# A gated linear attention with a feed-forward layer: the order of its pieces written anew, the state added by VectorE, the first logarithms split by ScalarE

## The chip, the cores and the metric

One core of one Trainium2 chip. The metric is the device time of one execution in microseconds (us), the median of the runs. Engines: TensorE (PE in the rows; PEld is its weight load), VectorE (DVE), ScalarE (ACT), GpSimd (POOL) and SyncE (SP), which issues most DMAs.

## The reference

```python
f = 1.0 / (1.0 + np.exp(-f_logit))            # B, H, S, D = 4, 8, 768, 48
for t in range(S):
    state = f[:, :, t, :, None] * state + einsum('bhd,bhe->bhde', k[:, :, t], v[:, :, t])
    y[:, :, t] = einsum('bhd,bhde->bhe', q[:, :, t], state)
x = y.transpose(0, 2, 1, 3).reshape(B * S, H * D)        # 3072 x 384
h = x @ w_in                                             # 384 -> 2048
out = (0.5 * (h + np.sqrt(h * h + 4.0))) @ w_out         # 2048 -> 384
```

## The kernel before, in words

The 3072 tokens are cut into 12 pairs of blocks, 256 tokens each, three pairs to a batch; a pair has two blocks of 128 tokens (cc = 0, 1), each on 64 partitions, two neighbouring tokens to a partition (i = 0, 1). All work is described as named pieces, `describe` makes them, and a table of words, ORDER, sets the order: the program emits the pieces in the order of the table. A word is the piece, the pair, a colon and the engine (A ScalarE, D VectorE, P GpSimd, S SyncE, T TensorE), for TensorE also the PSUM banks. So each engine takes its pieces in the table's order, and a piece that waits holds all that stands behind it on its engine.

The pieces of a pair p, with their lines in the kernel before:

- `lf`, `lq`, `lk`, `lv` (L171): loads of f, q, k, v, 384 KB each, issued by SyncE; `wi`, `wo` (L144, L149): the weights, issued by GpSimd.
- `ex` (L178): exp(-f). `ut` (L185): adds 1, into two of the three parts of the tile UT. `tt` (L138): their product. `ln` (L198, L202): its logarithm s. L138 is the helper of all multiplications, L133 and L135 of all copies.
- `hi`, `lo` (L208, L214): s as a fp16 high half and the remainder, in the tile hl. Pair 0 has none of both: it is in the list DIRECT, and its prefix sums run on the fp32 s32.
- `cu` (L234, L239): prefix sums of the logarithms by matmuls with a triangle, and sums of blocks. `c1` (L252, pairs 3 to 11): VectorE adds s for the second sum. `ep`, `ea`, `ge` (L262, L302): exponentials of the sums. `gs`, `gb` (L138): small factors of the state.
- `qu`, `ku`, `qm`, `km` (L138): q and k times factors. `vc`: v to fp16.
- `tp`, `te` or, for pairs 4 to 11, `tx` (L323): q and k transposed, on TensorE or by a DMA.
- `sc` (L364), `pm` (L371): scores and their mask. `kv` (L383): the pair's contribution to the state, in PSUM. `ia` (L394): a matmul of the old state sn with the identity, which adds it to `kv`'s result in PSUM. `sa`, `sb` (L401, L408): VectorE multiplies that sum with gs or gb, from PSUM, which gives the state for the next block.
- `yt` (L421), `yn` (L430): the output from within the block and from the state. `yc`: to fp16. `xp`, `xe` or, for pairs 4 to 11, `xx` (L445): y transposed.
- `m1` (L470), eight to a pair: h = y w_in, six matmuls each. `sq` (L479), `rt` (L485): square and square root on ScalarE. `gt` (L495): 0.5 h plus the root on VectorE. `m2` (L507), eight to a pair: four matmuls each of the output. `ev`, `st` (L527): copy and store.

Pair 0 is loaded and prepared in two halves of the heads (x = 0, 1: `ex0.0`, `ex0.1`). ScalarE switches between two tables of functions (the words TABLE:e and TABLE:s). The buffers of each tile rotate with the depths in DEPTH.

Of the kernel before, what the change touches and what calls it, by code (L numbers as in the profile page):

```python
# [31 lines left out]
ln2.0:A vc0.1:A lq2.0:S hi2.0:P pm0.00:D ep1.0:A gs0:P lo2.0:P ge1:A pm0.10:D vc0.0:A pm0.01:D ea1.0:A kv0:T@32 km1.0:P
ex3.0:A cu2.0:T@41 pm0.11:D lk2.0:S sa0:D yt0:T@60 ge2:A gs1:D yn0.1:T yc0.0:A qu1.0:D gb2:P lv1.0:S ep2.0:A qm1.0:D wi1:P
yc0.1:A ea2.0:A xp0.1:T@5 wi2:P xp0.0:T@7 ut3.0:D tp1.0:T@36 ex4.0:A lf5.0:S xe0.0:D tt3.0:P xe0.1:D te1.0.0:A te1.1.0:D
m1.0.0:T@4 wo3:P ln3.0:A ut4.0:D m1.0.1:T@0 wi3:P sq0.0:A qu2.0:D sc1.1:T@17 sq0.1:A hi3.0:P pm1.11:D TABLE:s rt0.0:A lo3.0:P
m1.0.2:T@5 pm1.10:D ia0.1:T lv2.0:S gb1:D cu3.0:T@3 tt4.0:D ku2.0:P sc1.0:T@67 sb0:D m1.0.3:T@1 pm1.00:D sq0.2:A pm1.01:D
# [5 lines left out]
pm2.01:D m1.1.5:T@0 hi4.0:P sq1.1:A lv3.0:S gt0.7:D lo4.0:P yt2:T@47 rt1.0:A gt0.6:D yn2.1:T m1.1.2:T@2 hi5.0:P sq1.3:A
gt1.1:D wo5:P m2.0.00:T@5 lf6.0:S sq1.2:A yc2.1:D m2.0.10:T@1 ku5.0:P rt1.1:A gt1.0:D m1.1.7:T@7 sq1.5:A gt1.3:D m1.1.6:T@3
sq1.7:A lo5.0:P yn2.0:T gt1.2:D lq4.0:S m2.0.11:T sq1.6:A km3.0:D m1.1.4:T@6 wo7:P rt1.3:A xp2.1:T@2 lf7.0:S m2.0.12:T wo6:P
qu3.0:D sq1.4:A m2.0.01:T xe2.1:D qm3.0:P yc2.0:A gt1.7:D cu4.0:T@2 rt1.2:A gt1.6:D xp2.0:T@4 m2.0.02:T TABLE:e ge4:A xe2.0:D
cu5.0:T@7 ku4.0:P gt1.4:D tp3.0:T@34 lq5.0:S c14.0:D m1.2.2:T@6 ex6.0:A te3.0.0:D m2.0.13:T vc3.0:P ep5.0:A gt1.5:D lf8.0:S
# [9 lines left out]
ev2.0:A ut9.0:D kv4:T@15 gb7:P st1.01.0:S sq3.0:A ia4.0:T tt8.0:D m2.2.12:T gs5:P ep7.0:A pm4.10:D m2.2.13:T ln8.0:A tt9.0:P
lq8.0:S sq3.1:A sa4:D yt4:T@32 gb5:P ln9.0:A ev2.1:D yn4.0:T vc5.0:P yn4.1:T lf11.0:S TABLE:s rt3.0:A m1.3.3:T@6 yc4.0:D
qu7.0:P yc4.1:D ia4.1:T sc5.0:T@17 sb4:D xx4:S kv5:T@32 qm6.0:P pm5.01:D ia5.0:T m1.3.2:T@5 sq3.3:A sa5:D m1.3.5:T@7 sq3.2:A
gt3.0:D km6.0:P m1.3.6:T@3 rt3.1:A gt3.1:D ia5.1:T m1.3.7:T@4 pm5.00:D sq3.5:A m1.3.4:T@2 gt3.2:D sq3.7:A ku7.0:P lk9.0:S
sc5.1:T@01 gt3.3:D sq3.4:A m2.3.10:T@5 st2.01.1:S rt3.2:A pm5.10:D lv7.0:S m1.4.2:T@6 pm5.11:D st1.01.1:S hi9.0:P m2.3.11:T  # L60
# [586 lines left out]
```

## Time and profile before

| | |
|---|---|
| median of 3 runs | 206.72 us (206.17 to 207.64) |
| the profiled execution | 205.34 us |
| its span, first to last instruction | 203.6 us |
| TensorE, VectorE, ScalarE, GpSimd busy | 177.7, 147.3, 154.9, 108.6 us |
| mean granted TensorE clock | 0.954 |
| moved by DMA | 32.87 MB, mean 161 GB/s |

Busy time is the time in which an engine has work, not work at its best: a busy share over the whole span is a mean over stages. Waits are what an engine stood idle for and what ended it. The chain is followed back from the last instruction, at each step to what released it. The clock row is in tenths of 2.4 GHz, 40 slices of 5.09 us.

### The profile page before, as it was taken

The page shows a single profiled execution, that of the slowest core. Times are in us where ns is not written, and L with a number is a line of the kernel's source. Part 1 is how long each engine was busy: PE and PEld are TensorE (multiplying, and loading weights), DVE is VectorE, ACT ScalarE, POOL GpSimd, SP SyncE. Part 2 cuts the span into 40 slices and gives each one's busy share as a digit, 9 for nine tenths or more (in the row PEclk, how much of TensorE's full clock was granted, in tenths as well). Part 3 has the DMA queues.
Part 4 walks back from the last instruction along what each step waited for, and adds up shares of the span by engine and source line. Part 5 has one row for each costly group of instructions (what it writes and reads, how often), then busy time and mean ns, then how long its engine had stood idle before and what let it go on. Part 6 is the DMA issues. An engine that isn't in the chain of part 4 may idle for free.

```text
span 203.6 us, 5630 instructions
## 1 busy us (share of the span) xinstructions
PE 177.7 (87%) x2302; PEld 129.1 (63%) x2302; DVE 147.3 (72%) x285; ACT 154.9 (76%) x248; POOL 108.6 (53%) x135
## 2 busy tenths in 40 slices
PE   0556898799899999979999979789998999999990
PEld 0544575587657766757667857467775778677660
DVE  7649579999688997957978958818984778434650
ACT  4266679999958999769988987758886698968700
POOL 4226789899969979929679738695000000000001
PEclk9995579999999999999999999969999999999998
DMA  6999999999959799994899999932894100505305
GB/s 158 269 262 244 275 198 217 234 256 273 183 156 234 108 254 203 222 278 99 129 214 207 249 129 240 195 51 36 149 140 119 39 5 0 42 0 155 77 22 136
DMA packets 80537, 32.87 MB, mean 161 GB/s; under 512 B 73888, under 2 KB 80496, under 8 KB 80512
## 3 DMA queue, kind: packets, MB, share of 16 engines
q1 hardware_dynamic: 76688, 29.27, 69.1%
q0 software_dynamic: 3824, 3.24, 9.9%
q8 instruction: 18, 0.29, 0.6%
q14 instruction: 7, 0.06, 0.1%
HBM read 25.17 MB, written 4.72 MB: 147 GB/s over the span
## 4 chain that ended last, share of the span: by engine, by line
issue 32%; PE 26%; POOL 18%; DMA 15%; ACT 3%; DVE 2%; SPq 2%; POOLq 0%
PE ps L507 10%; POOL qk L138 6%; PE ps L470 6%; DMA q<-in_q_dram 4%; PE ps L234 4%; POOL k L138 4%; DMA xT<-y 3%; DMA wout<-in_moe_w_out_dram 3%; DMA v<-in_v_dram 2%; POOL wout L149 2%; DMA f<-in_f_logit_dram 2%; POOL v L135 2%; POOL hl L214 2%; PE ps L364 1%; PE ps L383 1%
## 5 line engine op out<-in xcount | busy, mean ns | idle before, releaser
L470 PE MATMUL ps<-xT,win 128*128 128x256 f16 x576 | 74.0, 277 | 5.1 <-DMA xT<-y 3.5
L495 DVE SCALAR_TENSOR_TENSOR g<-ps,r 128x512 f16<-128x512 f32 x96 | 62.2, 682 | 17.5 <-ACT r L485 17.3
L507 PE MATMUL ps<-wout,g 128*128 128x384 f16 x384 | 71.6, 326 | 2.4 <-DMA wout<-in_moe_w_out_dram 1.3
L479 ACT ACTIVATE hsq<-ps 128x512 f16<-128x512 f32 x96 | 54.7, 593 | 18.0 <-PE ps L470 17.3
L470 PEld LDWEIGHTS <-win 128*128 128x128 f16 x576 | 55.5, 99 | 17.2 <-DMA xT<-y 4.2
L485 ACT ACTIVATE r<-hsq 128x1024 f16<-128x1024 f16 x48 | 50.6, 1056 | 1.1
L507 PEld LDWEIGHTS <-g 128*128 128x128 f16 x384 | 36.2, 98 | 22.6 <-issue 1.7
L371 DVE TENSOR_TENSOR pm<-ps,mask 128x512 f16<-128x512 f32 x48 | 30.8, 682 | 5.2 <-PE ps L364 5.0
L527 POOL DMA_DIRECT2D out_dram<-os x1 | 0.6, 602 | 59.7 <-ACT os L133 59.7
L138 POOL TENSOR_TENSOR qk<-q,ea 128x384 f16<-128x384 f32 x20 | 19.9, 1014 | 4.7 <-DVE q L138 4.7
L138 POOL TENSOR_TENSOR qk<-k,ep 128x384 f16<-128x384 f32 x20 | 19.8, 1013 | 0.3 <-ACT ge L302 0.2
L138 POOL TENSOR_TENSOR k<-k,UT 128x768 f32<-128x768 f32 x10 | 18.1, 1815 | 1.7 <-DMA k<-in_k_dram 1.6
L178 ACT ACTIVATE f<-f 128x768 f32<-128x768 f32 (+1 forms) x13 | 10.3, 795 | 3.3 <-DMA f<-in_f_logit_dram 3.2
L138 POOL TENSOR_TENSOR UT<-UT 128x384 f32<-128x384 f32 (+1 forms) x8 | 7.8, 984 | 8.9 <-DVE UT L185 8.9
L214 POOL TENSOR_TENSOR hl<-s,hl 128x384 f16<-128x384 f32 x11 | 10.0, 912 | 4.8 <-ACT hl L133 4.7
L133 ACT COPY os<-ps 128x384 f32<-128x384 f32 x12 | 5.8, 480 | 8.6 <-PE ps L507 7.2
L401 DVE TENSOR_TENSOR sn<-ps,gs 128x384 f16<-128x384 f32 x12 | 6.6, 554 | 7.7 <-PE ps L383 5.3
L135 POOL CAST v<-v 128x768 f16<-128x768 f32 x10 | 8.2, 821 | 5.2 <-DMA v<-in_v_dram 5.2
L364 PE MATMUL ps<-qkT 48*64 48x128 f16 x384 | 9.4, 228 | 0.7 <-ACT qkT L133 0.6
L135 DVE COPY os<-ps 128x384 f32<-128x384 f32 x12 | 6.5, 552 | 4.8 <-PE ps L507 3.1
L262 ACT ACTIVATE ep<-ps 128x384 f32<-128x384 f32 (+1 forms) x13 | 6.0, 470 | 5.2 <-PE ps L239 5.0
L364 PEld LDWEIGHTS <-qkT 48*64 48x64 f16 x384 | 6.4, 110 | 4.9 <-issue 3.5
(74 smaller groups left out, 200.8 us busy)
## 6 DMA issues: line engine op xcount, KB each, us to landing
f<-in_f_logit_dram SPq DMA_DIRECT2D x11, 384.0 KB, 6.2
k<-in_k_dram SPq DMA_DIRECT2D x11, 384.0 KB, 5.4
q<-in_q_dram SPq DMA_DIRECT2D x11, 384.0 KB, 6.2
v<-in_v_dram SPq DMA_DIRECT2D x11, 384.0 KB, 5.2
out_dram<-os SPq DMA_DIRECT2D x22, 192.0 KB, 3.5
win<-in_moe_w_in_dram POOLq DMA_DIRECT2D x4, 384.0 KB, 7.5
wout<-in_moe_w_out_dram POOLq DMA_DIRECT2D x8, 192.0 KB, 6.5
f<-in_f_logit_dram SPq DMA_DIRECT2D x2, 192.0 KB, 2.9
```

The lines of the kernel that those rows point to most:

```text
L135: eng(e).tensor_copy(out=o, in_=i)
L138: eng(e).tensor_tensor(out=o, in0=a, in1=b, op=ALU.mult)
L178: nc.scalar.activation(out=t, in_=t, func=AF.Exp, scale=-1.0)
L214: eng(e).tensor_tensor(out=hl[:, 1, hs, 0:D], in0=T["s", p][:, hs], in1=hl[:, 0, hs, 0:D], op=ALU.subtract)
L234: nc.tensor.matmul(out=o, lhsT=tri[:, m], rhs=t[:, hs, 0:D], start=(r == 0), stop=(r == len(terms) - 1))
L364: nc.tensor.matmul(out=T["sc", p, i, h][64 * cc:64 * cc + 64, j, :], lhsT=t[r, 1, j, i, :], rhs=t[r, 0, j], start=True, stop=True)
L371: nc.vector.tensor_tensor(out=T["pm", p, i, h], in0=T["sc", p, i, h], in1=K["mask"][:, i].unsqueeze(1).broadcast_to([128, 4, 128]), op=ALU ...
L470: nc.tensor.matmul(out=T["h", p, m][:, a], lhsT=K["win"][m // 2][:, j, m % 2 * 256 + a * 128:m % 2 * 256 + a * 128 + 128], rhs=T["xT", p][ ...
L479: nc.scalar.activation(out=T["hsq", p, r][:, a], in_=T["h", p, m].rearrange("p a c t -> p (a c t)"), func=AF.Square, scale=1.0)
L485: nc.scalar.activation(out=T["r16", p, r], in_=T["hsq", p, r], func=AF.Sqrt, scale=0.25, bias=1.0)
L495: nc.vector.scalar_tensor_tensor(out=T["g", p][:, 2 * m:2 * m + 2, :].rearrange("p a t -> p (a t)"), in0=T["h", p, m].rearrange("p a c t - ...
L507: nc.tensor.matmul(out=T["o", p, cc], lhsT=T["g", p][:, jn, cc * 128:(cc + 1) * 128], rhs=K["wout"][jn // 2][:, jn % 2, :], start=(jn == 0 ...
```

## The change

1. The table ORDER is written anew for all engines; the costs in `describe` change for the DMA transposes only. Many words also name another engine than before: km1, km2, ku5 to ku7 and lo1, lo2, lo4, lo8 go from GpSimd to VectorE; tt2, tt4, tt8, qm1, qu1, qu2, qu3, qu5 and gb1 from VectorE to GpSimd; hi2 from GpSimd to ScalarE, and so on.
2. Pairs 3 to 11 (the new list SADD) have no `ia`. A new piece `sp` on VectorE adds the old state to `kv`'s result from PSUM, into an fp32 tile st in SBUF; `sa` or `sb` multiplies st with the factor, now on GpSimd for all twelve of them. A sum that no later block reads (the last of a batch) is not made any more: `ia` goes from 20 pieces to 5 (pairs 0 to 2), `sp` has 12.
3. Pair 0 leaves DIRECT: its sums are fp16 with `hi` and `lo` like the others'. ScalarE makes `hi0` as a logarithm straight from UT, in fp16 (HI_ACT); `lo0` is on VectorE and on GpSimd. The fp32 copies of the triangle and of ind and the tile s32 are no longer made, and the triangle is built with four instructions in place of eight.
4. The last two stores are issued by SyncE, those before them (st11.0) by GpSimd.

Lists and branches that stay unused (SPLIT, PMACT) are left out here, and of ORDER one line of each is shown.

```diff
-DIRECT = [0]
+DIRECT = []
+SADD = [3, 4, 5, 6, 7, 8, 9, 10, 11]
+HI_ACT = [0]
...
 ORDER = """
-lf0.1:S lf0.0:S lf1.0:S lk0.0:S lk0.1:S TABLE:e ex0.1:A lq0.1:S ut0.1:D ex0.0:A tt0.1:D lq0.0:S ut0.0:D lf2.0:S tt0.0:P
+lf0.0:S lf0.1:S lk0.1:S lf1.0:S lk0.0:S TABLE:e ex0.0:A lq0.0:S ut0.0:D ex0.1:A tt0.0:P lq0.1:S ut0.1:D hi0.0:A lv0.0:S
...
+                    direct = p in HI_ACT
+
+                    def hi(e, bk, x=x, hs=hs, p=p, direct=direct):
+                        o = K["hl"][p % NHL][:, 0, hs, 0:D]
+                        if direct:
+                            nc.scalar.activation(out=o, in_=T["UT", p][:, 1, hs], func=AF.Ln)
+                        else:
+                            copy(e, o, T["s", p][:, hs])
...
-                for m in mats:
-                    o = T["cum", p, m][:, h0 * D:h1 * D]
                     for r, t in enumerate(terms):
-                        nc.tensor.matmul(out=o, lhsT=tri[:, m], rhs=t[:, hs, 0:D], start=(r == 0), stop=(r == len(terms) - 1))
+                        for m in mats:
+                            nc.tensor.matmul(out=T["cum", p, m][:, h0 * D:h1 * D], lhsT=tri[:, m], rhs=t[:, hs, 0:D],
+                                             start=(r == 0), stop=(r == len(terms) - 1), skip_group_check=True)
...
-            if cc == 0 and first:
-                pass
-            else:
+            added = p in SADD
+            if not (cc == 0 and first) and not added:
                 def ia(e, bk, cc=cc, p=p):
...
+            if cc == 1 and (p + 1) % 3 == 0:
+                continue
...
+            if added and not (cc == 0 and first):
+                def sp(e, bk, cc=cc, p=p):
+                    T["st", p, cc] = sb(f"st{cc}", p, [128, 4, 2, 48], FP32)
+                    nc.vector.tensor_tensor(out=T["st", p, cc], in0=T["u", p, cc], in1=T["sn", p, cc], op=ALU.add)
...
+                def sm(e, bk, cc=cc, p=p, nxt=nxt, factor=factor):
+                    T["sn", nxt[0], nxt[1]] = sb(f"sn{1 - cc}", nxt[0], [128, 4, 2, 48], FP16)
+                    mul(e, T["sn", nxt[0], nxt[1]], T["st", p, cc], factor())
```

What the table changes on the engines is seen at three places. First ScalarE from the start to the first copies of q and k (f becomes its exponential, UT the product; s and hl are the logarithms, ep, ea and ge the exponentials of the sums in ps). Before:

```order
L178 ACTIVATE f<-f 128x384 x2
L178 ACTIVATE f<-f 128x768
L198 ACTIVATE s_109<-UT 128x4x48 x2
L262 ACTIVATE ep<-ps_159 128x192
L262 ACTIVATE ea<-ps_160 128x192 x2
L302 ACTIVATE ge<-ps_159 128x12
L262 ACTIVATE ep<-ps_159 128x192
L202 ACTIVATE s<-UT 128x384
```

The same place in the changed kernel:

```order
L182 ACTIVATE f<-f 128x384 x2
L259 ACTIVATE hl_91<-UT 128x4x48
L249 ACTIVATE s<-UT 128x192
L259 ACTIVATE hl_91<-UT 128x4x48
L249 ACTIVATE s<-UT 128x192
L182 ACTIVATE f<-f 128x768
L313 ACTIVATE ep<-ps_151 128x192
L313 ACTIVATE ea<-ps_152 128x192
L313 ACTIVATE ep<-ps_151 128x192
L249 ACTIVATE s<-UT 128x384
L313 ACTIVATE ea<-ps_152 128x192
```

Two more logarithms stand ahead of the sums; the exponential of pair 1 (128x768) moves behind them, and the logarithm of pair 1 ahead of the last exponential of pair 0.

Second VectorE at the state of pairs 4 and 5, before (sn is the new state, pm a masked score, y the output of a pair, os a result to be stored, g the activation):

```order
L371 TENSOR_TENSOR pm_1604<-ps_1472,mask 128x512
L401 TENSOR_TENSOR sn_1616<-ps_1571,gs 128x384
L135 COPY os<-ps_1551 128x384
L135 CAST y_1679<-ps_1618 128x384
L135 CAST y_1679<-ps_1619 128x384
L408 TENSOR_TENSOR sn_1702<-ps_1572,gb 128x384
L371 TENSOR_TENSOR pm_1726<-ps_1685,mask 128x512
L401 TENSOR_TENSOR sn_1738<-ps_1706,gs 128x384
```

The same place in the changed kernel (st is the sum before its multiplication):

```order
L469 TENSOR_TENSOR st_1592<-ps_1553,sn_1509 128x384
L430 TENSOR_TENSOR pm_1598<-ps_1476,mask 128x512
L430 TENSOR_TENSOR pm_1625<-ps_1600,mask 128x512
L430 TENSOR_TENSOR pm_1635<-ps_1601,mask 128x512
L469 TENSOR_TENSOR st_1678<-ps_1554,sn_1623 128x384
L139 COPY os<-ps_1503 128x384
L139 CAST y_1697<-ps_1645 128x384
```

The multiplications are gone from VectorE; the second addition reads sn_1623, which GpSimd makes.

Third GpSimd at the same place, changed kernel:

```order
L142 TENSOR_TENSOR sn_1509<-st_1305,gb 128x384
L142 TENSOR_TENSOR gs<-ge,half 128x24
L142 TENSOR_TENSOR UT<-UT 128x384 x2
L142 TENSOR_TENSOR sn_1623<-st_1592,gs 128x384
L142 TENSOR_TENSOR gs<-ge,half 128x24
L142 TENSOR_TENSOR qk_95<-q,ea 128x4x2x48 x2
L142 TENSOR_TENSOR q<-q,UT 128x8x48
L142 TENSOR_TENSOR gb<-gs,ge 128x8
L139 CAST v_1742<-v 128x768
L142 TENSOR_TENSOR sn_1758<-st_1678,gb 128x384
```

Three multiplications of the state (sb3, sa4, sb4) stand here between the products of pairs 6, 8 and 9 and the cast of v of pair 5; in the kernel before GpSimd has none of them.

## Rows read from the trace of the kernel before

**Rows 1.** The page, parts 1 and 2: busy us per engine, POOL and clock in 40 slices

```profile
PE 177.7 (87%) x2302; PEld 129.1 (63%) x2302; DVE 147.3 (72%) x285; ACT 154.9 (76%) x248; POOL 108.6 (53%) x135
...
POOL 4226789899969979929679738695000000000001
...
PEclk9995579999999999999999999969999999999998
```

**Rows 2.** Waits of PE from 27 us on: us in total, times, longest

```profile
PE ps L470 <- DMA xT<-y: 3.5, 2, 2.0
PE ps L470 <- DMA win<-in_moe_w_in_dram: 1.7, 3, 0.9
PE ps L507 <- DMA wout<-in_moe_w_out_dram: 1.3, 2, 1.0
PE ps L507 <- DVE g L495: 1.1, 1, 1.1
PE ps L383 <- ACT os L133: 0.8, 1, 0.8
PE ps L383 <- POOL v L135: 0.5, 1, 0.5
```

**Rows 3.** Timeline, 0 to 42 us: start us, us, engine, line, operation, out<-in, count

```profile
4.48 0.52 ACT L178 ACTIVATE f<-f 128x384 f32<-128x384 f32 x1 [0.51 <-DMA f<-in_f_logit_dram]
...
5.23 0.36 DVE L138 TENSOR_TENSOR UT<-UT 128x192 f32<-128x192 f32 x1
...
5.94 0.59 POOL L138 TENSOR_TENSOR UT<-UT 128x192 f32<-128x192 f32 x1 [2.88 <-DVE UT L185]
...
7.06 0.60 ACT L198 ACTIVATE s<-UT 128x192 f32<-128x192 f32 x2
...
26.11 2.39 PE L470 MATMUL ps<-xT,win 128*128 128x256 f16 x12
...
29.88 0.49 PE L234 MATMUL ps<-hl,tri 128*128 128x384 f16 x2
...
30.20 0.34 PE L239 MATMUL ps<-ind,hl 128*128 128x3 f16 x8
```

**Rows 4.** Chain that ended last, in order of time: start us, us, what

```profile
7.46 2.93 PE ps L234 x8
10.38 1.12 PE ps L239 x8
...
22.60 0.44 POOL gb L138
...
49.77 6.55 DMA wout<-in_moe_w_out_dram
...
63.73 0.16 PE ps L394
...
77.62 0.27 PE ps L394
```

**Rows 5.** Groups by line and shape: busy us, mean ns | idle before, releasers

```profile
L138 POOL TENSOR_TENSOR qk<-q,ea 128x384 f16<-128x384 f32 x20 | 19.9, 1014 | 4.7 <-DVE q L138 4.7
...
L394 PE MATMUL ps<-sn,ident 128*128 128x384 f16 x20 | 6.8, 339 | 0.1
...
L401 DVE TENSOR_TENSOR sn<-ps,gs 128x384 f16<-128x384 f32 x12 | 6.6, 554 | 7.7 <-PE ps L383 5.3 <-PE ps L394 2.3
```

**Rows 6.** Chain and PE timeline: two late arrivals of xT

```profile
81.06 6.93 DMA xT<-y
...
133.21 0.93 PE L470 MATMUL ps<-xT,win 128*128 128x256 f16 x6 [2.00 <-DMA xT<-y]
```

**Rows 7.** Timeline, last 5 us

```profile
199.74 0.60 POOL L527 DMA_DIRECT2D out_dram<-os  x1 [59.66 <-ACT os L133]
```

**Rows 8.** Line L138 and tile gs: ns min/median/max, first and last start

```profile
L138 POOL TENSOR_TENSOR qk<-q,ea x20: 986/998/1314, 34.0 to 139.1; 128x384 f16<-128x384 f32 x20
...
L138 DVE TENSOR_TENSOR gb<-gs,ge x3: 155/677/923, 30.1 to 146.1; 128x8 f32<-128x8 f32 x3
```

More of the change, by code (lines that the diff above doesn't have):

```diff
@@ L32 @@
[L32 to L36, printed above, removed]
@@ L42 @@
[L42 to L46, printed above, removed]
@@ L56 @@
[L56 to L60, printed above, removed]
@@ new lines @@
+tt0.1:D ln0.0:A hi0.1:A lo0.0:D lf2.0:S ln0.1:A ku0.1:D cu0.0:T@01 ex1.0:A lo0.1:P ku0.0:D cu0.1:T@01 ep0.0:A lk1.0:S km0.0:D
+qu0.0:P ut1.0:D ea0.1:A lq1.0:S ep0.1:A tt1.0:D qu0.1:D ln1.0:A qm0.1:D lv0.1:S ea0.0:A km0.1:D ex2.0:A qm0.0:D tp0.1:T@23
+hi1.0:A lf3.0:S ut2.0:D tp0.0:T@23 ge0:A te0.1.1:A lo1.0:D tt2.0:P te0.1.0:A te0.0.1:D cu1.0:T@45 lf4.0:S te0.0.0:A ku1.0:D
+lk2.0:S wi0:P ln2.0:A sc0.1:T@67 sc0.0:T@10 ge1:A vc0.0:A gs0:P pm0.10:D qu1.0:P hi2.0:A lq2.0:S pm0.01:D vc0.1:A wi2:P
+lo2.0:D ea1.0:A kv0:T@32 pm0.11:D ex3.0:A cu2.0:T@60 qm1.0:P pm0.00:D ep1.0:A ea2.0:A sa0:D lv1.0:S yt0:T@57 km1.0:D yn0.1:T
@@ new lines @@
+m2.2.12:T sq3.1:A sa4:P pm5.10:D ln9.0:A lk7.0:S m2.2.13:T pm5.11:D gs6:P TABLE:s rt3.0:A qm6.0:P yt4:T@46 sp4.1:D yn4.0:T
+ev2.1:D yn4.1:T m1.3.5:T@7 yc4.1:D sc5.0:T@23 qu8.0:P ev2.0:D m1.3.4:T@6 yc4.0:A gt3.1:D sq3.5:A xx4:S m1.3.3:T@1 gb5:P
+vc5.0:P pm5.00:D sq3.4:A m1.3.2:T@4 rt3.2:A pm5.01:D sb4:P lq7.0:S kv5:T@02 lf10.0:S gt3.0:D yt5:T@23 sq3.3:A gb7:P yn5.0:T
+hi9.0:P lv7.0:S sp5.0:D m1.3.6:T@5 sq3.2:A km6.0:P gt3.4:D rt3.1:A m2.3.00:T@0 yc5.0:D lv6.0:S m1.3.7:T@6 sq3.6:A gt3.2:D
+m1.4.1:T@2 hi8.0:P sq3.7:A gt3.3:D m1.4.2:T@4 lo9.0:P lk8.0:S rt3.3:A gt3.5:D m1.4.0:T@1 gs7:P sq4.1:A gs5:P m2.3.01:T gt3.6:D
@@ L180, in describe @@
                   cost={"A": 0.2 + 0.84e-3 * 2 * n})
-            def ut(e, bk, x=x, hs=hs, p=p):
-                if ("UT", p) not in T:
-                    T["UT", p] = sb("UT", p, [128, 3, 8, 48], FP32)
-                eng(e).tensor_scalar(out=T["UT", p][:, 0::2, hs], in0=T["f", p][:, hs].rearrange("p h i d -> p i h d"),
-                                     scalar1=1.0, scalar2=None, op0=ALU.add)
-            W.add(f"ut{p}.{x}", "D", ut, reads=[f"e{p}.{x}"], makes=[f"u{p}.{x}"], uses=[("f", p), ("UT", p)],
-                  lock=True, cost={"D": 0.05 + 0.83e-3 * 2 * n})
@@ L241, in describe @@
-            need = xs if last else [x]
-            sides = [f"s{p}.{y}" for y in need] if p in DIRECT else [f"{w}{p}.{y}" for w in ("lo", "hi") for y in need]
-            full = 0.67 if p not in DIRECT else 1.4
-            W.add(f"cu{p}.{x}", "T", cu, reads=sides, makes=[f"cum{p}.{x}"], uses=[("s32", p) if p in DIRECT else ("hl", p)],
-                  banks=[f"cx{p}"] + ([] if p in ADD1 else [f"c1{p}"]), mode="F",
-                  cost={"T": full * len(mats) / 2 * nh / 8 + ((0.24 if p not in DIRECT else 0.5) if last else 0.0)})
@@ L257, in describe @@
-            for m, nm, sgn in ((0, "ep", 1.0), (1, "ea", -1.0)):
-                def xp(e, bk, m=m, nm=nm, sgn=sgn, x=x, hs=hs, h0=h0, h1=h1, p=p):
-                    if (nm, p) not in T:
-                        T[nm, p] = sb(nm, p, [128, 8, 48], FP32)
-                    t = T[nm, p][:, hs].rearrange("p h d -> p (h d)")
-                    nc.scalar.activation(out=t, in_=t if m == 1 and p in ADD1 else T["cum", p, m][:, h0 * D:h1 * D], func=AF.Exp, scale=sgn)
-                if m == 1 and p in ADD1:
-                    W.add(f"{nm}{p}.{x}", "A", xp, reads=[f"cumi{p}.{x}"], makes=[f"{nm}{p}.{x}"], uses=[(nm, p)], table="e",
-                          cost={"A": 0.2 + 0.85e-3 * n})
-                else:
-                    W.add(f"{nm}{p}.{x}", "A", xp, reads=[f"cum{p}.{x}"], makes=[f"{nm}{p}.{x}"],
-                          uses=[(nm, p), ("bank", f"c{'x1'[m]}{p}")], table="e", cost={"A": 0.17 + 0.85e-3 * n})
@@ L270, in qu @@
-            def qu(e, bk, x=x, hs=hs, p=p):
-                t = T["q", p][:, hs, 0, :]
-                mul(e, t, t, T["UT", p][:, 2, hs])
-            W.add(f"qu{p}.{x}", "DP", qu, reads=[f"q{p}.{x}", f"u{p}.{x}"], makes=[f"qu{p}.{x}"], uses=[("q", p), ("UT", p)],
-                  lock=True, cost={"D": 0.14 + 1.1e-3 * n, "P": 0.1 + 2.3e-3 * n})
-            def ku(e, bk, x=x, hs=hs, p=p):
-                t = T["k", p][:, hs].rearrange("p h i d -> p i h d")
-                mul(e, t, t, T["UT", p][:, 0:2, hs])
@@ L615 @@
             e, _, banks = rest.partition("@")
+            if name.startswith("wm"):
+                t = ps(banks, [128, 128], FP32)
+                for n in range(int(name[2:])):
+                    nc.tensor.matmul(out=t, lhsT=ident, rhs=ident, start=True, stop=True)
+                continue
             W.pieces[name].emit(e or W.pieces[name].eng, banks)
```

394 lines of the change are left out of this document (243 added, 151 removed).

## The prediction

> **What bounds the kernel now.** I read the page's busy times first. TensorE (PE) is busy 177.7 of 203.6 us, VectorE (DVE) 147.3, ScalarE (ACT) 154.9, GpSimd (POOL) 108.6 [rows 1]. No share says "bound" by itself, so next came PE's waits from 27 us on: six kinds, 3.5 + 1.7 + 1.3 + 1.1 + 0.8 + 0.5 = 8.9 us in all [rows 2]. So from its first big matmul at 26.11 us [rows 3] to the last, PE works for nearly the whole time, and the end moves by three things: when that first matmul starts, how much PE work follows, and how long PE waits in between. The chain of waits shows what sets the start: eight fp32 matmuls (L234, 2.93 us) and eight small ones (L239, 1.12 us), from 7.46 to 11.50 us, on an otherwise idle PE, with ScalarE's exponentials waiting behind them [rows 4]. POOL's row shows a second fact: 9 and 8 tenths through slices 6 to 18 (28 to 92 us), and nothing after 140 us [rows 1]. It feeds the early pairs of row blocks, and has slack late.
>
> **Term 1, the start.** Pair 0 no longer uses fp32 logarithms. I follow the new order by hand. The second exponential of pair 0 ends at 4.48 + 0.52 = 5.00 us [rows 3]. The add of 1 costs 0.36 (taken like the product of the same half), the product 0.36: 5.72. Now ScalarE takes hi0.0, ln0.0, hi0.1, ln0.1. One half is 0.60 / 2 = 0.30 us in the pipelined pair, about 0.35 alone, so the last logarithm ends at 5.72 + 2 x 0.35 = 6.4. The remainder lo0.1 is on POOL, 0.59 like the POOL product of a half [rows 3]: 7.0, with semaphores 7.1. The prefix sums are now fp16: the two-matmul group of a later pair took 0.49 and the eight small ones 0.34 [rows 3], together 0.83, so pair 0 has its sums at 7.9 us instead of 11.50: 3.6 us earlier. Part of that is lost before the first big matmul. VectorE now takes km0.0, ut1, tt1 and two more pieces before the last product of pair 0, so ScalarE's ln1.0 waits for tt1 with ea0.0 behind it. lo1, lo2 and km1 come to VectorE in this stretch, while tt2, qu1 and qm1 go to POOL. The load of lk0.1 stands before lf1.0. I charge 0.9 us for this and keep **-2.7 us**. Ends: -3.6 (nothing lost) and -1.0: the q and k loads, which VectorE and POOL wait for here in before, may hold pair 0, and the granted clock stands at 5 tenths (1.2 of 2.4 GHz) in slices 3 and 4, 15 to 25 us [rows 1]; if it rises no sooner, matmuls that start 2.7 us earlier give 1.4 us back.
>
> **Term 2, PE work.** The ia piece, an identity matmul that adds the state into PSUM, goes from 20 to 5. On the chain one costs 0.16 to 0.27 us of PE's stream [rows 4]. The 339 ns mean of its group [rows 5] includes the drain under the next matmul and is only the far end. 15 x 0.17 = **-2.5 us**; ends -2.4 and -5.1. The rest of PE's pieces keep their number. Twelve additions (sp) take the place on VectorE, from PSUM; I price one like the state's multiplication from PSUM, 0.554 us [rows 5], so 6.6 us. Twelve multiplications leave VectorE for POOL, worth the same 6.6 there and 12 x 1.014 = 12.2 us on POOL, by the nearest row, a product of two tensors of 128x384 [rows 5]. VectorE's sum is unchanged. POOL's would come to 118 with what else moves (three ku and four lo leave it, three qu and three tt come): 58% of the span. At zero for the end, since POOL is idle from 140 us on [rows 1], so the late multiplications fall into free time. Without that cover each costs 1.0 us plus what POOL is doing.
>
> **Term 3, PE's waits.** The new order keeps the distance between a transpose of y and the first matmul on it at 2.9 to 8.5 us of PE work for pairs 4 to 11 (counted in pieces at 0.66 us), before 3.1 to 11.3. One arrival took 6.93 us, and another left PE waiting 2.00 us [rows 6]. Of the weights, win2 is issued behind less POOL work than before, the other three win behind somewhat more (0.7 to 2.7 us), and wout3, which stood before win3, now comes with the other wout. I see fewer close calls at pairs 4 and 7 and new ones at pairs 6 and 10, and take **0**. Ends: -4.6, if the waits for xT and g go (3.5 + 1.1 [rows 2]), and +4, one more late arrival at each of two close pairs at 2.0.
>
> **Term 4, the tail.** Both last stores now stand on SyncE one behind the other, where POOL had one (issue 0.60 us [rows 7]). One issue more in line, at most +0.6, against POOL's later start; taken as 0.
>
> **A rule against the change.** VectorE's gb piece took from 155 to 923 ns, the middle one of three 677, for 8 elements a partition [rows 8]. Such a small piece cannot work that long: it stood behind something, and POOL's product of the same kind ranges from 986 to 1314 ns [rows 8]. Both read two tensors from SBUF. The Trainium skill (SBUF — State Buffer, section "SBUF: two separate sides") calls it an exclusive lock: a VectorE instruction with two SBUF inputs and a GpSimd instruction share one port pair, and the later blocks fully. The rows agree in kind. By that rule the twelve new POOL multiplications and the two-input pieces that come to VectorE (three ku, five lo, one more km) get in each other's way. In rows: about ten such pieces come to VectorE and about a dozen leave it (gb, gs, tt, qu, qm), so VectorE's exposure hardly changes. POOL's twelve products at the worst surplus, 1314 - 998 = 0.32 us, would be 12 x 0.32 = 3.8 us late, if all of it reached PE. I take 0 and keep it as a rival.
>
> **The sum.** The profiled execution took 205.34 us (span 203.6 and 1.7 around it). 205.34 - 2.7 - 2.5 + 0 + 0 = 200.1 us. The median of the runs is 206.72, 1.4 higher, so the forecast for a median is 206.72 - 5.2 = **201.5 us**, 2.5% faster.
>
> **Rivals.**
> A. The waits go too. For it: VectorE's wait for a late q load and PE's for xT are single events, and pair 7's sums now stand well ahead. Against: nothing makes DMAs faster. 201.5 - 4.6 = 196.9 us.
> B. The front stays bound by POOL. For it: from 22.60 to 49.77 us the chain is nearly all POOL [rows 4], and up to the first output matmul the new order puts about 2 us more on POOL (qm1, qm3, qu1 to qu3, tt2, tt4, two wout issues in; km1, km2, ku3, lo1, lo2, lo4, hi2, hi4 out) for 1.5 us more of PE work. Against: most of POOL's pieces start earlier with the start. Then term 1 is given back: 206.72 - 2.5 = 204.2 us.
> C. The port of SBUF, as above: 201.5 + 3.8 = 205.3 us.
> D. Slower: the state's chain becomes the bound at pairs 3 to 5. The next state now needs an addition on VectorE and then a multiplication on a full POOL: sa4 stands there behind tt8 and tt9, sb4 behind qm6, qu8 and vc5, which waits for a load. Four steps (sa3, sa4, sb4, sa5) have only 1.0 to 2.0 us of PE work up to the yn matmul that reads them; the other eight mostly 4 to 20 us. The waiting yn holds all that stands behind it on PE, m1 and m2 pieces, and so ScalarE. A fully exposed step costs 0.55 + 1.0 - 0.17 - 0.55 = 0.8 plus a running product pair of 2.0, 2.8 us. Three of the four: 201.5 + 8.4 = 209.9 us. It makes the change slower from the second step on (2 x 2.8 = 5.6 against 5.2 won). Against: kv and sp are written some pieces ahead of these yn, and POOL's other pieces there wait for little.
>
> **How the numbers follow.** My forecast, with 199.5 to 203.5 about it, 0.47; A 0.20; B 0.13; C 0.08; D 0.12. About 1% is what a measurement of this kernel can tell from no change, so faster means under 204.65 and slower over 208.8. Faster: 0.47 + 0.20 + 0.07 of B = 0.74. Same: 0.06 of B and 0.08 of C = 0.14. Slower: D, 0.12. The range takes in A and C and leaves out D: 196.5 to 206.5.
>
> **What would show it.** Right: the first big matmul (L542 in the changed kernel) at 23.4 us, between 22.5 and 25; the fp16 sums of pair 0 over at about 7.9 us; five identity matmuls left; PE's waits from there on still 7 to 10 us in sum; the last matmul near 193.7. B shows as a first matmul at 23 to 24 us, followed by waits on pieces behind POOL before 60 us. C shows as POOL products with means clearly over 1014 ns. D shows as PE waiting in the yn group for POOL's sn between 70 and 95 us. The forecast is wrong if PE's waits after the first matmul sum to over 13 us or under 5.

## The result, and the profile after

The changed kernel takes 196.09 us (median of 4 runs, 195.20 to 196.87) against 206.44 us (205.95 to 207.64): ratio 0.9489, 95% interval 0.9429 to 0.9549. The forecast was 201.5 us with a range of 196.5 to 206.5: the direction was right, and the time lies 0.4 us below the range. The control run below, the same kernel on another chip, took 196.5 us, the edge of the range, with a ratio of 0.9616 [0.9562, 0.967]. Medians in the table of runs are, like the ratios, over undisturbed executions (two of six in e2, three of six in e16), while the profiles of e2, e4, e7, e13 and e16 are of disturbed ones. The kernel before had 204.8 to 206.7 us from chip to chip, so between runs of different chips a difference is given by medians and by ratios; the two can be 1% apart.

The profiled execution took 196.35 us, with a span of 194.1. The page, part 1, then PE's waits from the first big matmul on (us in total, times, longest; answers to [rows 1, 2]):

```profile
PE 171.3 (88%) x2287; PEld 123.7 (64%) x2287; DVE 151.8 (78%) x278; ACT 156.3 (81%) x250; POOL 117.3 (60%) x150
```

```profile
PE ps L542 <- DMA win<-in_moe_w_in_dram: 2.2, 3, 1.0
PE ps L415 <- DMA qkT<-qk: 1.1, 2, 0.7
PE ps L542 <- DMA xT<-y: 1.1, 2, 0.6
PE ps L542 <- DVE os L139: 0.8, 1, 0.8
PE ps L443 <- DVE pm L430: 0.5, 2, 0.4
PE ps L284 <- DVE g L567: 0.5, 1, 0.5
PE ps L415 <- DVE qkT L139: 0.4, 1, 0.4
PE ps L493 <- DVE g L567: 0.3, 1, 0.3
PE ps L415 <- DVE sn L142: 0.3, 1, 0.3
PE ps L579 <- DVE g L567: 0.2, 1, 0.2
```

The sum is 7.4 where it was 8.9, and made of other waits: those on xT fell from 3.5 to 1.1, and wout is gone. The groups that changed (by line and shape, columns as in [rows 5]):

```profile
L142 POOL TENSOR_TENSOR qk<-q,ea 128x384 f16<-128x384 f32 x22 | 22.2, 1034 | 0.1
L469 DVE TENSOR_TENSOR st<-ps,sn 128x384 f32<-128x384 f32 x12 | 6.6, 552 | 0.9 <-POOL sn L142 0.4 <-PE ps L443 0.2
L142 POOL TENSOR_TENSOR sn<-st,gs 128x384 f16<-128x384 f32 x6 | 5.0, 829 | 13.1 <-DVE st L469 13.0
L453 PE MATMUL ps<-sn,ident 128*128 128x384 f16 x5 | 1.6, 330 | 0.1
```

Five identity matmuls are left, the additions cost VectorE the 6.6 us of the forecast, and the multiplications GpSimd 0.83 us each, not 1.01.

PE's timeline at the start, first before (columns as in [rows 3]), then after:

```profile
14.67 0.58 PE L340 MATMUL ps<-ident,qk 64*128 64x64 f16 x15 [0.33 <-ACT qkT L133]
15.90 1.34 PE L364 MATMUL ps<-qkT 48*64 48x128 f16 x32 [0.65 <-ACT qkT L133]
17.17 1.46 PE L234 MATMUL ps<-hl,tri 128*128 128x384 f16 x4
...
19.88 0.82 PE L383 MATMUL ps<-v,qk 64*128 64x96 f16 x16 [1.05 <-ACT v L133]
```

```profile
7.42 0.40 PE L290 MATMUL ps<-ind,hl 128*128 128x3 f16 x8
11.46 1.84 PE L391 MATMUL ps<-ident,qk 64*128 64x64 f16 x32 [3.65 <-DVE qk L142]
13.24 1.46 PE L284 MATMUL ps<-hl,tri 128*128 128x384 f16 x4
...
14.99 1.07 PE L415 MATMUL ps<-qkT 48*64 48x128 f16 x32
...
16.70 0.67 PE L443 MATMUL ps<-v,qk 64*128 64x96 f16 x12 [0.37 <-ACT v L137]
...
21.98 1.49 PE L542 MATMUL ps<-xT,win 128*128 128x256 f16 x12 [0.36 <-DMA win<-in_moe_w_in_dram]
...
188.81 0.81 PE L579 MATMUL ps<-wout,g 128*128 128x384 f16 x4
```

Pair 0's sums end at 7.42 + 0.40 = 7.82 us (11.50 before), its transposes at 13.30 (15.25), and the first big matmul starts at 21.98 (26.11). The sums of pair 1 (L284) now run at 13.24, while ScalarE and VectorE copy the transposes; before, they stood behind the scores (L364). The last matmul ends at 188.81 + 0.81 = 189.6 us, forecast near 193.7.

To see where the time went I gave each moment of PE's stream between first and last big matmul to the instruction in it, or to waiting, and summed by kind (worked out from the two traces):

| us | before | after | forecast | measured |
|---|---|---|---|---|
| first big matmul at | 26.11 | 21.98 | -2.7 | -4.1 |
| identity matmuls | 4.0 | 1.3 | -2.5 | -2.7 |
| PE's waits and gaps | 9.1 | 7.8 | 0 | -1.3 |
| big matmuls (m1 and m2) | 130.5 | 129.2 | 0 | -1.3 |
| the rest of PE's work | 29.3 | 29.4 | 0 | +0.1 |
| tail (last m2 to the span's end) | 4.7 | 4.5 | 0 | -0.2 |
| around the span | 1.7 | 2.2 | 0 | +0.5 |
| sum | | | -5.2 | -9.0 |

The control's trace, summed in the same way, has its first big matmul at 22.87 us (-3.2), identity matmuls -2.8, waits and gaps 5.8 (-3.2) and big matmuls 130.4 (-0.1). So the identity matmuls are firm, while the other three shift among each other by 0.9 to 2 us from one execution of the same kernel to another.

### The profile page after: what moved, and what is told of

It reads as the page before. It is cut to its first block, busy times and chain, and to the rows that moved or that the text cites. A ratio compares the mean times of both kernels' runs of the same rounds, so it can differ in the third digit from the quotient of the medians.

```text
span 194.1 us, 5593 instructions
## 1 busy us (share of the span) xinstructions
PE 171.3 (88%) x2287; PEld 123.7 (64%) x2287; DVE 151.8 (78%) x278; ACT 156.3 (81%) x250; POOL 117.3 (60%) x150
## 4 chain that ended last, share of the span: by engine, by line
PE 54%; DMA 21%; POOL 9%; DVE 9%; SPq 2%; issue 2%; ACT 1%; DVEq 0%; POOLq 0%
PE ps L579 23%; PE ps L542 21%; DMA win<-in_moe_w_in_dram 4%; DMA wout<-in_moe_w_out_dram 4%; DMA qkT<-qk 4%; DMA k<-in_k_dram 3%; DMA v<-in_v_dram 2%; DMA xT<-y 2%; PE ps L415 2%; PE ps L493 2%; DVE pm L430 2%; DVE qk L142 2%; POOL qk L142 2%; DMA out_dram<-os 2%; PE ps L502 2%
## 5 line engine op out<-in xcount | busy, mean ns | idle before, releaser
L542 PEld LDWEIGHTS <-win 128*128 128x128 f16 x576 | 54.5, 98 | 16.2 <-DMA win<-in_moe_w_in_dram 2.9
L142 POOL TENSOR_TENSOR qk<-q,ea 128x384 f16<-128x384 f32 x22 | 22.2, 1034 | 0.1
L142 POOL TENSOR_TENSOR qk<-k,ep 128x384 f16<-128x384 f32 x18 | 17.6, 1002 | 0.2
L142 POOL TENSOR_TENSOR UT<-UT 128x384 f32<-128x384 f32 (+1 forms) x11 | 11.3, 1031 | 9.1 <-DVE UT L232 8.6
L284 PE MATMUL ps<-hl,tri 128*128 128x384 f16 (+1 forms) x34 | 9.1, 377 | 6.4 <-ACT hl L259 5.5
L142 POOL TENSOR_TENSOR sn<-st,gs 128x384 f16<-128x384 f32 x6 | 5.0, 829 | 13.1 <-DVE st L469 13.0
L142 POOL TENSOR_TENSOR k<-k,UT 128x768 f32<-128x768 f32 x7 | 12.6, 1812 | 0.0
L142 POOL TENSOR_TENSOR q<-q,UT 128x384 f32<-128x384 f32 (+1 forms) x10 | 10.3, 1033 | 2.6 <-DMA q<-in_q_dram 2.4
L139 DVE COPY os<-ps 128x384 f32<-128x384 f32 x14 | 7.6, 551 | 4.5 <-DMA out_dram<-os 2.2
L232 DVE TENSOR_SCALAR UT<-f 128x768 f32<-128x768 f32 (+1 forms) x13 | 8.8, 687 | 1.2 <-ACT f L182 1.1
```

The costliest lines, as they stand in the source:

```text
L139: eng(e).tensor_copy(out=o, in_=i)
L142: eng(e).tensor_tensor(out=o, in0=a, in1=b, op=ALU.mult)
L232: eng(e).tensor_scalar(out=T["UT", p][:, 0::2, hs], in0=T["f", p][:, hs].rearrange("p h i d -> p i h d"), scalar1=1.0, scalar2=None, op0=A ...
L284: nc.tensor.matmul(out=T["cum", p, m][:, h0 * D:h1 * D], lhsT=tri[:, m], rhs=t[:, hs, 0:D], start=(r == 0), stop=(r == len(terms) - 1), sk ...
L542: nc.tensor.matmul(out=T["h", p, m][:, a], lhsT=K["win"][m // 2][:, j, m % 2 * 256 + a * 128:m % 2 * 256 + a * 128 + 128], rhs=T["xT", p][ ...
```

## The experiments

| run | us | ratio to before |
|---|---|---|
| e0, the changed kernel again | 196.5 | 0.9616 [0.9562, 0.967] |
| e1, new order, state edit undone | 199.0 | 0.9651 [0.9591, 0.9711] |
| e2, new order, fp32 sums back | 197.6 | 0.9573 [0.9495, 0.965] |
| e16, new order, both undone | 202.6 | 0.9839 [0.9748, 0.993] |
| e3, old order, fp16 sums alone | 204.5 | 0.9867 [0.9806, 0.9928] |
| e4, old order, state edit alone | 208.5 | 1.0114 [1.0049, 1.0179] |
| e5, old order, both edits | 205.7 | 0.9948 [0.9902, 0.9995] |
| e6, cu1.0 moved back | 203.0 | 0.983 [0.9763, 0.9897] |
| e7, multiplications on VectorE | 198.4 | 0.9636 [0.9559, 0.9713] |
| e8, two win loads earlier | 198.3 | 0.9611 [0.9552, 0.967] |
| e9, km2.0 moved | 196.4 | 0.9616 [0.9558, 0.9674] |
| e10, e8 and km2.0 moved | 196.8 | 0.9633 [0.9582, 0.9684] |
| e11, e6 and km2.0 moved | 198.3 | 0.9698 [0.9621, 0.9775] |
| e12, before, cu1.0 moved forward | 205.1 | 0.9948 [0.9904, 0.9991] |
| e13, e5, cu1.0 moved forward | 202.9 | 0.9859 [0.979, 0.9928] |
| e14, e7 and km2.0 moved | 197.7 | 0.9643 [0.956, 0.9727] |
| e15, e2 and km2.0 moved | 198.3 | 0.969 [0.9612, 0.9768] |

**The order and the two edits.** e1 to e5 and e16 are the corners: each order with neither edit, one, or both.

```diff
 e1
-SADD = [3, 4, 5, 6, 7, 8, 9, 10, 11]
+SADD = []
 e2
-DIRECT = []
-HI_ACT = [0]
+DIRECT = [0]
+HI_ACT = []
```

In e1 the words sp become ia (twelve more), the twelve sa and sb read PSUM on VectorE right behind them, and gs5 and gb5 move up on their engine, to where their reader is. e3 to e5 put the edits into the old ORDER: hi0 and lo0 added (e3, e5); ia to sp, and sa, sb to GpSimd (e4, e5). e16 does in the new order what e1 and e2 do.

> The changed kernel with the identity matmuls back in pairs 3 to 11 (17 in all; the three that no block reads stay out), the state's multiplication on VectorE from PSUM right behind each, no addition on VectorE. Theory (PE's stream is the bound, each ia costs it what the trace before shows, 4.0 us for 20, 0.2 each): 12 x 0.2 = 2.4 us slower than the changed kernel, ratio to before about 0.960. Rival (the sum on VectorE was worth nothing, its chain over POOL gave back what PE won): within 0.5 us of the changed kernel, ratio about 0.949, or below.

> The changed kernel with pair 0 back on fp32 sums (DIRECT), all else in the new order. Theory (the start passes whole to the end): pair 0's sums end 3.7 us later, near 11.5 us, first big matmul near 25.7, and the end 3.7 us later: ratio to before about 0.967. Rival (the weights are what the first matmuls wait for, 2.2 us of waits on win in the changed kernel's trace, so they take up a late start): 1.5 us slower than the changed kernel, ratio about 0.956.

> The old order, with one part alone: pair 0's sums in fp16, high halves by ScalarE. Theory (the start passes whole to the end): sums end 3.6 us earlier, the end 3.6 us earlier, ratio about 0.983. Rival (in the old order GpSimd's front and the weights hold PE up to 56 us whenever the start comes): under 1.5 us won, ratio above 0.993.

> The old order, with one part alone: no identity matmul in pairs 3 to 11, the state added by VectorE and multiplied by GpSimd at the places of the old ia, sa and sb. Theory (PE's stream is the bound): 15 x 0.2 = 3 us won, ratio about 0.986. Rival (the state's chain is longer, and in an order not made for it GpSimd's multiplications stand behind long products, so PE's yn waits): not faster, ratio 1.00 to 1.03.

> The old order with both edits of the code: fp16 sums of pair 0, and the state added by VectorE and multiplied by GpSimd. What is left to the changed kernel (ratio 0.949) is then the order's own part. Theory (terms add up): 3.6 + 3 us won, ratio about 0.968, and the order's own part about 4 us. Rival (the edits need the new order): ratio above 0.985, the order's part over 7 us.

> The new order without both edits: ia back in pairs 3 to 11 (17 ia, sa and sb on VectorE from PSUM; gs5, gb5, gb10 a little earlier), fp32 sums of pair 0 back. Theory (the order carries nearly all, the edits add their 3.2 and 1.8 us): 196.5 + 3.2 + 1.8 = 201.5, between 200.5 and 203.5, about 0.975 to 0.985 of before. Rival (the order pays only because the edits take work off it): 204.5 to 207, no different from before.

By ratios the order alone gives 1.6%, the edits in the old order 0.5%, and both together 3.8 to 5.1%: the parts don't add. The fp16 sums are worth 1.3% in the old order and 0.8% in the new one (e15 against e0; 1.8 us, 0.9%, by medians), about the same. Both are less than expected. In e3 pair 0's sums end at 10.39 us, 1.1 earlier than before and not 3.6. In e2 the fp32 sums end at 8.34 + 1.71 = 10.05 us, not at 11.5, because the new order alone starts them at 5.62 us (7.46 before). Its first big matmul, at 23.34 us, comes 1.4 us after that of the changed kernel, not 3.7.

```profile
5.62 2.93 PE L282 MATMUL ps<-s,tri 128*128 128x192 f32 x8 [5.62 <-ACT s L243]
8.34 1.71 PE L288 MATMUL ps<-ind,s 128*128 128x3 f32 x8
```

It is the state edit that turns: 1.1% slower in the old order (e4; e5 against e3 0.8%), faster in the new one, by 2.5 us or 1.2% by medians and 0.4% by ratios (e1 against e0). The 0.4% lies within the intervals. The profile of e1 agrees with the larger figure: its identity matmuls take 3.4 us of PE's stream for 1.3, and its last matmul ends at 192.3 us, 2.2 behind the control's 190.1.

The profile of e5 against that of before shows where the edit's gain is lost in the old order: PE's waits and gaps are 12.2 us for 9.1, as much more as the identity matmuls give (1.1 us for 4.0). The big matmuls and the rest of PE's work take another 2.3 us more there, which is not explained. PE's longest waits in e5 from 24 us on, and ScalarE's timeline at the second:

```profile
PE ps L540 <- DMA xT<-y: 3.8, 2, 2.6
PE ps L441 <- ACT os L135: 2.9, 1, 2.9
PE ps L577 <- DMA wout<-in_moe_w_out_dram: 1.6, 1, 1.6
```

```profile
156.84 0.48 ACT L135 COPY os<-ps 128x384 f32<-128x384 f32 x1 [3.51 <-DMA out_dram<-os]
```

What PE saves in the old order it gives back at the next arrivals, a transposed y and a store that ScalarE's copy waits for (a PSUM bank, and with it pair 11's contribution to the state, waits for that copy). The same wait on os is 0.8 us in the kernel before and 1.6 in e3, where only the sums are edited; so it can grow without the state edit. The new order has no wait on os of more than 0.8 us, none on xT over 0.6. That the later arrivals come from the twelve multiplications on GpSimd no row shows; this link is open, and so is where e4 loses, whose longest wait is another (3.6 us, on win).

A part of what the order alone lacks may be a hold of VectorE by GpSimd, of the kind shown below. In e16's profile VectorE's lo4.0, 0.67 us in the control, takes 3.44 us, and PE waits for the masked scores behind it; e2 and e7 have the same (3.59 and 3.50 us). No run takes this hold out of e16.

```profile
43.24 3.44 DVE L265 TENSOR_TENSOR hl<-s,hl 128x384 f16<-128x384 f32 x1
47.34 1.13 PE L540 MATMUL ps<-xT,win 128*128 128x256 f16 x6 [2.09 <-DVE pm L428]
```

**One word at the start.**

```diff
 e6, PE's words; e12 and e13 do the reverse in the old order
-te0.0.1:D cu1.0:T@45 ... sc0.1:T@67 sc0.0:T@10
+te0.0.1:D ... sc0.1:T@67 sc0.0:T@10 cu1.0:T@45
```

> The changed kernel with one word moved: on TensorE pair 1's prefix sums (cu1) stand behind pair 0's scores again, as before, no longer ahead of them. Theory (that move is why the first big matmul came 1.4 us earlier than forecast, the sums of 1.7 us lie beside the copies of q and k): first big matmul 1.0 to 1.5 us later, near 23.2, the end later by 0.5 to 1.5, ratio to before 0.952 to 0.957. Rival (the copies and the mask set the pace, not TensorE): first big matmul within 0.4 us of 21.98, ratio 0.949.

> The kernel before with one word moved: cu1.0 from behind sc0.1 to ahead of sc0.0 on PE. Theory (this place is a part of its own of what the new order gains): the sums of pair 1 run beside the copies of pair 0's transposes, PE's waits of 0.65 us there and of 1.05 us on v go, and the first big matmul starts 1.0 to 2.0 us earlier; time 0.990 to 0.996 of the kernel before. Rival (it pays only with the rest of the new order): first big matmul within 0.5 us of before's, time the same.

> The old order with both edits, and cu1.0 ahead of sc0.0. Theory: the first big matmul 1.0 to 2.0 us earlier than the 24.72 us of the old order with both edits, and the time by as much: 204 to 205, about 0.985 to 0.99. Rival: same as without the word, 0.995, since the later waits (xT, v, wout) take it up.

e6 starts its first big matmul at 24.76 us, 2.8 later than the changed kernel and 1.9 later than the control. From the end of pair 0's transposes (13.70) that is 11.1 us; the changed kernel needs 8.7 and the kernel before 10.9.

```profile
11.85 1.85 PE L389 MATMUL ps<-ident,qk 64*128 64x64 f16 x32 [4.07 <-DVE qk L140]
...
24.76 1.47 PE L540 MATMUL ps<-xT,win 128*128 128x256 f16 x12 [0.23 <-DVE xT L137]
```

In the kernel before the word alone brings 0.7 us there (25.39, less than expected) and with the edits 1.3 (23.42 for 24.72). In e12 what is left is one wait, of pair 0's contribution to the state on the cast of v:

```profile
15.51 1.46 PE L232 MATMUL ps<-hl,tri 128*128 128x384 f16 x4
...
19.16 0.82 PE L381 MATMUL ps<-v,qk 64*128 64x96 f16 x16 [1.00 <-ACT v L131]
```

In the changed kernel ScalarE casts all of v ahead of pair 1's exponentials, and the wait is 0.37; no run varies that alone. But e6 lost 6.5 us against the control (4.4 by ratios), more than its start. PE's timeline in e6 shows a wait that the changed kernel has with 0.50 us, and VectorE's and GpSimd's show its cause:

```profile
34.11 0.82 PE L282 MATMUL ps<-hl,tri 128*128 128x384 f16 x2 [3.15 <-DVE g L565]
```

```profile
28.65 4.80 DVE L140 TENSOR_TENSOR qk<-k,ep 128x384 f16<-128x384 f32 x2
29.07 1.01 POOL L140 TENSOR_TENSOR UT<-UT 128x384 f32<-128x384 f32 x1
30.03 0.92 POOL L265 TENSOR_TENSOR hl<-s,hl 128x384 f16<-128x384 f32 x1
30.89 1.20 POOL L137 CAST v<-v 128x768 f16<-128x768 f32 x1
32.05 0.98 POOL L140 TENSOR_TENSOR q<-q,UT 128x384 f32<-128x384 f32 x1
```

km2.0, two products of two SBUF inputs each, takes 4.80 us on VectorE, and gt0.0, whose g PE needs, stands behind it. The first product alone held from 28.65 to 31.41 us. VectorE's masks pm, larger but with one input in PSUM, kept their time in the same trace, all 48 of them (ns min/median/max):

```profile
28.65 2.76 DVE L140 TENSOR_TENSOR qk<-k,ep 128x384 f16<-128x384 f32 x1
L428 DVE TENSOR_TENSOR pm<-ps,mask x48: 674/681/693, 16.1 to 163.7; 128x512 f16<-128x512 f32 x48
```

Behind PE's wait the granted clock stands at 5 tenths (1.2 of 2.4 GHz), where the control's is full. The stretch, with PE's busy time, the clock, the DMA share and GB/s:

```profile
34.00:40.80 6.80, 6.69 (x109) 0.50 1.26 258
```

So e6 is behind the control by 1.9 us at the first big matmul, by 4.2 at the sums of pair 3 (34.11 for 29.90), by 5.4 at the end of this stretch (40.83 for 35.40) and still by 5.4 at its last matmul (195.50 for 190.09). The pieces of the hold in the control run:

```profile
27.41 0.92 POOL L267 TENSOR_TENSOR hl<-s,hl 128x384 f16<-128x384 f32 x1
28.23 1.02 DVE L142 TENSOR_TENSOR qk<-k,ep 128x384 f16<-128x384 f32 x2
29.46 0.82 POOL L139 CAST v<-v 128x768 f16<-128x768 f32 x1 [1.13 <-DMA v<-in_v_dram]
```

Here GpSimd waits 1.13 us for the load of v, and km2.0 takes 1.02. In e1 that wait is 0.95 and km2.0 1.43, in the changed kernel 0.73 and 1.89; in e2, e6, e7, e8 and e16 there is no such wait, and km2.0 takes 2.04 us (e16) to 4.80.

**The hold of km2.0.** e8 issues wi2 and wi1 earlier, since PE waits 2.2 us on win; e7 gives the twelve multiplications to VectorE. In both km2.0 was held (3.46 and 2.96 us), as in e2 (3.85). e9, e10, e11, e14 and e15 move km2.0 to where GpSimd issues DMAs. Of the twelve words of e7 three are shown.

```diff
 e8
-wi0:P ... gs0:P ... qu1.0:P ... wi2:P ... qm1.0:P ... gb1:P ... wi1:P
+wi0:P wi2:P ... gs0:P ... qu1.0:P ... wi1:P qm1.0:P ... gb1:P
 e9, and on top of e6, e7, e8, e2: e11, e14, e10, e15
-wi3:P km2.0:D sq0.5:A ... gt0.0:D ... yc1.0:D
+wi3:P sq0.5:A ... gt0.0:D ... yc1.0:D km2.0:D
 e7
-sb3:P ... sa4:P ... sb4:P
+sb3:D ... sa4:D ... sb4:D
```

> The changed kernel with the twelve multiplications of the state on VectorE instead of GpSimd, same places. Theory (neither engine bounds where they stand; VectorE is at 78% and goes to 81%): within 1 us of the changed kernel, ratio 0.946 to 0.954. Rival 1 (GpSimd's relief of VectorE carries the gain): over 2 us slower, ratio above 0.959. Rival 2 (the shorter latency, 0.55 instead of 1.0 us, helps): 1 us faster, ratio below 0.944.

> The changed kernel with two words moved: GpSimd issues win2 right behind win0 and win1 ahead of qm1, about 1 and 2.4 us earlier. Theory (the 0.98 and 0.83 us that TensorE waits for win at 24.6 and 27.6 us are late issues): both waits under 0.3 us, the end 1 to 1.6 us earlier, ratio to before 0.941 to 0.944. Rival (the DMA engines are full from 5 us on, so weights that come earlier push loads back): waits move to loads, the end within 0.5 us, ratio 0.949.

> The changed kernel itself, on the chip of the next three, as their yardstick. Expected 0.949 of the kernel before, with VectorE's km2.0 (the two products of k and ep at 27 us) at about 1.9 us and no wait for it at the sums of pair 3.

> The changed kernel with one word moved: km2.0 from before gt0.0 to behind yc1.0 on VectorE, where GpSimd issues DMAs. Theory (GpSimd's pieces hold VectorE's products): km2.0 takes 1.0 to 1.2 us in place of 1.89, gt0.0 comes 1.9 us earlier, the 0.5 us wait of PE on g at the sums of pair 3 goes, and the time is 0.3 to 1.0 us less than the changed kernel's. Rival (the duration of km2.0 has nothing to do with GpSimd, or PE waits anyway): km2.0 still 1.9 us, time the same within 0.3 us, or later because the transposes of pair 2 wait for km2.0.

> The run with the two win loads issued earlier, and km2.0 behind yc1.0 as well. Theory: the 2.3 us wait of PE on VectorE's g at the sums of pair 3 and the half clock behind it go, while the shorter waits on win (1.0 in place of 2.2 us) stay: 2 to 3.5 us less than that run's 198.9, so 195.4 to 196.9, level with the changed kernel or 1 us better. Rival (the loads cost elsewhere, the hold of km2.0 was only beside it): still over 198, with the wait at another piece.

> The run with cu1.0 behind sc0.0 on PE, and km2.0 behind yc1.0 as well. Theory: of the 5.9 us that the last matmul came later, 2.8 are the start and about 3.1 the wait on g behind km2.0 (4.80 us); the start stays late, the wait goes: the last matmul at 192.0 to 193.0, time 199.0 to 200.5, ratio 0.965. Rival (the late start is passed on and multiplied by other waits): still 0.98, km2.0 short but PE waiting as long for something else.

> The changed kernel with the twelve multiplications of the state on VectorE, and km2.0 behind yc1.0. Theory (half of the 3 us that this edit cost was the hold of km2.0, 2.96 us there): the 1.5 us wait of PE on g at the sums of pair 3 goes and the time falls from 198.4 to 196.9 or less, within 0.3% of the changed kernel. Rival (the relief of VectorE is the whole of it): still 198 to 199.5, with waits of PE on VectorE's pm.

> The changed kernel with the fp32 sums of pair 0 back, and km2.0 behind yc1.0. Theory: the first big matmul stays 1.4 us late (23.3), the 1.7 us wait on g goes; time 197.8 to 199.0 where it was 201.0 (197.6 in the best of its runs). Rival (the later start costs more than itself elsewhere): 200 or more.

e11 separates the two parts of e6: the start stays at 24.72, 1.9 us behind the control's 22.87, but the wait on g goes, the last matmul ends at 192.58 instead of 195.50, and the median falls from 203.0 to 198.3 (the profiled executions from 202.1 to 199.5). So the word's own place is worth about 1.8 us by the medians, and the hold of km2.0, with the half speed behind it, made 2.7 to 4.7. The 1.8 is not the start alone: e11's profile has two stretches at half speed of its own (30.1 to 33.4 and 40.3 to 43.6 us). e10 brings e8 from 198.3 to 196.8, no better than the control: the earlier loads leave 0.3 us of waits on win, but km2.0 is now the last before its own transposes:

```profile
PE ps L391 <- DVE qk L142: 1.6, 1, 1.6
```

e9 changes nothing (196.4), because in the control the hold hardly occurs (1.02 us). e14 is 1.1 us above the control (0.3% by ratios, within the intervals) with km2.0 still at 2.56 us, so what GpSimd's relief of VectorE is worth isn't told apart from nothing. No run beat the changed kernel by more than the measurement can tell.

## Why the prediction was wrong

**Term 1** is the step that failed first. The sums of pair 0 came when forecast, 7.82 for 7.9. Behind them I wrote "I charge 0.9 us for this". Up to the end of pair 0's transposes the loss was double: of 3.68 us there 1.95 were left (13.30 for 15.25). But from there to the first big matmul 2.2 us were won (8.7 for 10.9), and the term came to -4.1, in the control to -3.2. I had listed ScalarE's, VectorE's and GpSimd's words and not PE's: with cu1.0 behind the scores (e6) nothing of the 2.2 is left, and the term is -1.4 (24.76 for 26.11). So the pieces behind the sums that I had listed cost 2.3 of the 3.7 us and not 0.9, and one I had not listed gave 1.9 to 2.8 back. That -2.7 lies between is luck. By e11 the word is worth 1.8 us of the time.

**The clock.** I gave 1.4 us back in Term 1's low end, if it rises no sooner. In the profiled execution the first 12 big matmuls took 1.49 us for 2.39, which is 0.9 of the -1.3 of the big matmuls. The stretch at half speed (133.9 to 137.2 us, the 6 of [rows 1]) that followed the 2.00 us wait of [rows 6] is gone too; its share isn't told apart. This size isn't firm: in the control the first 12 took 2.74 us, as long as at half speed, though the page's clock row has 9 tenths and more there. Its profiled execution was only 0.5 us slower, because its waits and gaps sum to 5.8.

```profile
22.87 2.74 PE L542 MATMUL ps<-xT,win 128*128 128x256 f16 x12 [0.72 <-DMA win<-in_moe_w_in_dram]
```

**Term 2** held: -2.7 for -2.5, five identity matmuls, 6.6 us of additions. VectorE's sum, taken as unchanged, rose from 147.3 to 151.8 us; GpSimd's came to 117.3 for 118. GpSimd's multiplications were 0.83 us, 10 in sum for the 12.2 I took. **Term 3** was taken as 0 and was -1.3, in the control -3.2. The waits' sum of 7.4 lies in the 7 to 10 I gave as right, the control's 5.7 does not; the xT part fell by 2.4 and others came. **Term 4** was right (-0.2).

**The step from execution to median** was wrong by 1.6: I added the 1.4 us by which the execution before lay under its median, while after lies 0.26 above its own. This is scatter between executions and no mechanism. The rest of the 5.4 us, 3.8, are the terms above.

**Rival A** came nearest in time (196.9), but the waits gave only 1.3 of its 4.6 (3.2 in the control). **B** did not happen as I priced it; up to 60 us PE waited for no piece of GpSimd, and 2.2 us for win, whose loads GpSimd issues (1.7 before). **D** did not either: sp waited 0.4 us in all for GpSimd's sn (group L469), and PE never. Its sign was right where I hadn't looked, in the old order (e4), but not by PE's wait in the yn group for GpSimd's state. **C** I priced at 0 here and by GpSimd's products; those stayed near 1014 ns (1034). The price sits on the other engine: VectorE's product waits, 1.02 us for km2.0 where GpSimd paused longest, 2.04 to 4.80 where it did not. By the rule of the Trainium skill (SBUF — State Buffer, section "SBUF: two separate sides") a VectorE instruction with two SBUF inputs and a GpSimd instruction that reads SBUF share a port pair under an exclusive lock, and the runs agree in kind. That moving km2.0 takes back most of what e6 lost beyond its start shows the piece. That it is the port was not varied by itself; that only pieces with two SBUF inputs stretch (last section) speaks for it.

## What to carry to other kernels

Judge an edit in the order in which it will run: the state edit was 1.1% slower in one and 0.4 to 1.2% faster in the other. Follow the engine that waits through its own list of pieces too, not only those that feed it. A VectorE piece with two SBUF inputs just ahead of something urgent is a risk beside a busy GpSimd: with GpSimd's UT product starting 0.9 us ahead of it (changed kernel) km2.0 took 1.89 us, with both starting together (e8) 3.46. The profile of the good case does not show this. Profile the same kernel twice before pricing a start, a wait or a clock: here they shifted by 0.9 to 2 us.

## What the runs showed of the hardware that I had not expected

Which pieces of VectorE can be held shows in all 19 traces together. Its TENSOR_TENSOR pieces of 128x384 with one input in PSUM took 540 to 559 ns, all 551 of them; those of the same size with both inputs in SBUF took 539 to 3592 ns (283 of them).

VectorE's hold outlasts one GpSimd instruction. In e6 the first product of km2.0 was there from 28.65 us on, and two GpSimd pieces (UT and hl) began and ended before it finished at 31.41; before the second finished at 33.45, the cast of v and the product q had ended too. GpSimd's cast, with one input, took 1.20 us there for 0.82 in the control.

A wait seems to have kept the changed kernel fast at this place: beside the same GpSimd pieces km2.0 took 1.02 to 1.89 us in the profiles in which GpSimd waited 0.73 to 1.13 us for a late load of v, and 2.04 to 4.80 in those without that wait. No run moves the load alone.
